# A list-scheduled Fourier and maxout kernel: its plan counts loads, issues and shared PSUM reads in another way

## The chip, the cores and the metric

The kernel runs on one NeuronCore of one Trainium2 chip. The metric is the device time of one execution in microseconds, the median of several runs. PE is TensorE (matmuls), DVE VectorE, ACT ScalarE, POOL GpSimd, SP SyncE; each runs its own instructions in the order in which they stand in its queue.

## The reference

```python
X = np.fft.rfft(x, axis=1)                       # x: 8 x 3072 x 256, float32
Yr = Xr @ w_r - Xi @ w_i + b_r                   # 256 x 256 weights
Yi = Xr @ w_i + Xi @ w_r + b_i
Y* = sign(Y*) * max(|Y*| - 0.01, 0)
y = np.fft.irfft(Yr + 1j * Yi, n=3072, axis=1)   # float32
x = y.reshape(8 * 3072, 256)
h = max(max(x @ w1, x @ w2), x @ w3)             # 256 x 768 weights
return h @ w_out                                 # 768 x 256
```

## The kernel before

For each of 8 batches the Fourier transform is done as matmuls in stages. **Stage a** loads a piece `xq` of x (8 pieces a batch), takes its largest value (`mxx`, DVE, which sets a scale later), multiplies by a small DFT table (`pa`), copies to `aq` (ACT) and writes it to DRAM (`a_d`). **Steps k = 0 to 11** load a slab `aj` of `a_d`, split it into a float16 pair `ah`, `al`, multiply (`px`), split that (`tt`, and a sum `s`), multiply with w_r and w_i (`py`), add the bias and threshold (`u`, `t`), split (`vp`), transform back (`pz`), copy to `zs` (ACT) and write to DRAM (`z_d`). **The second part** takes 8 chunks c a batch: load `zp` from `z_d` (one buffer; GpSimd clears its middle rows, then SP issues two loads), split it into `zh` (ACT) and `zl` (DVE), multiply (`pi`), split into `yh`, `yl`. Then, for six slices f of a chunk, the maxout layer: `pu` (two PSUM tiles of 12 matmuls in all; w3 is taken off the other two weights beforehand and added back in `pd`), `c1` (ACT, called c in the profile), `h32` (DVE, h in the profile), the pair `hh` (ACT then DVE), and `pd`, from which `o` is copied out by ACT and written by DMAs that ACT issues. Nearly every product is three float16 matmuls (`mm3`: lines 304 to 306 before); L298 and L299 are the helper that splits.

A **slot** is one (batch, chunk, slice), 48 a batch and 384 in all. Slots are counted here by c1: "c1 number 98" is batch 2, chunk 0, slice 2. The second part of batch b runs beside the first part of batch b + 1; `at` and `run_until` place a step's functions in the slots.

The code is traced in that written order, and what comes after the mark (from slot 6 on) is then put in another order by a planner. `gather` groups instructions into operations with a cost (`busy`) and a time until others may use the result (`wait`), from the tables `COST`. `link` finds what each operation needs (`needs`) or must stand behind (`behind`): who wrote what it reads, and who used a buffer that it takes over (`BUFS` gives the number of buffers). `arrange` plays all of it through, and picks for DVE and ACT the ready operation that is due first, for PE the first ready one within 40 in the written order; POOL, and before the change SP, stay as written. The order that comes out is fixed by dependencies that cost no semaphore. No time of this planner is used in this document: it fixes the order, and the chip decides how long things take.

In the plan before, `link` made only the **first** writer of a reused buffer wait for the buffer's former users. For `xq` and `zp` that is GpSimd's memset, so their loads waited for nothing there. A DMA that ACT issues counted 0.13 us of ACT. ACT and DVE reads of one PSUM tile did not wait for each other in the plan (the program itself does order them).

Of the kernel before, what the change touches and what calls it, by code (L numbers as in the profile page):

```python
# [24 lines left out]
def dft_tables():  # L25
# [57 lines left out]
    def halves(v, scale):  # L83
# [20 lines left out]
    "DVE": {  # L104
        "h32": 0.475, "hh": 0.475, "yl": 0.467, "zl": 1.2, "t": 0.45, "mxu": 0.6, "mxx": 0.6, "vp": 0.66, "s": 0.36,
        "al": 0.67, ("u", 256): 0.49, ("u", 512): 0.605, ("tt", 512): 0.605, ("tt", 256): 0.34,
    },
    "Activation": {
        "c1": 0.43, "hh": 0.43, "yh": 0.37, "o": 0.36, "ah": 0.61, "zh": 1.04, "zs": 0.6, "vp": 0.6, "s": 0.37,
        "cs": 0.37, "aq": 0.493, ("tt", 512): 0.48, ("tt", 256): 0.3,  # L110
    },
}


class Op:
    def __init__(self, engine, label, key=None):
        self.engine, self.label, self.key = engine, label, key
        self.ins, self.reads, self.writes, self.busy = [], set(), set(), 0.0


def gather(traced):
    ops, last = [], None
    for i in traced:
        ends = [[a for a in v if getattr(a, "bass_ap", None) is not None] for v in (i.ins, i.outs)]
        if not ends[1]:
            continue
        reads, writes = ([a.bass_ap.tensor.name for a in v] for v in ends)
        sizes = [int(np.prod([c for _, c in a.ap[1:]])) for v in ends for a in v]
        engine, n = str(i.engine).split(".")[-1], sizes[-1]
        label = writes[0].rsplit("_", 1)[0]  # L130
        if engine == "PE":
            key = label if label in ("pi", "pa", "pd") else writes[0]
            if last is None or last.key != key:
                last = Op(engine, label, key)
                last.busy = {"pi": 0.19, "pa": 0.1}.get(label, 0.0)
                ops.append(last)
            plain = ends[0][0].dtype == F32
            cost = (4 if plain else 1) * n / 2400 + 0.0025
            last.busy += {"pi": cost / 2, "pa": 0.23}.get(label, cost)
            last.wait = last.busy + 0.22  # L140
            op = last
# [12 lines left out]
        op.writes |= set(writes)  # L154
    return ops


def link(ops):
    wrote, read, taken, used, opened = defaultdict(list), defaultdict(list), defaultdict(list), set(), {}
    reuse = []  # L160
    for k, o in enumerate(ops):
        o.needs, o.behind = {w for t in o.reads for w in wrote[t]}, set()
        for t in o.writes:
            name = t.rsplit("_", 1)[0]
            if name not in ("a_d", "z_d"):
                o.needs |= set(read[t])
            tag = TAGS.get(name, name)
            if t not in used:
                used.add(t)
# [3 lines left out]
                if len(taken[tag]) > BUFS.get(tag, 2):  # L173
                    reuse.append((k, taken[tag][-1 - BUFS.get(tag, 2)]))
# [25 lines left out]
def arrange(ops, first):  # L200
# [6 lines left out]
    left, ready = [len(kept & (o.needs | o.behind)) for o in ops], [0.0] * len(ops)  # L207
    free, order, open_ = defaultdict(float), defaultdict(list), defaultdict(list)
    written = defaultdict(list)
    for k, o in enumerate(ops):  # L210
# [4 lines left out]
    done, count = defaultdict(int), len(ops) - len(kept)  # L215
    ran = [False] * len(ops)
    while count < len(ops):
        best = None
        for e, c in open_.items():
            if not c:  # L220
                continue
            w = written[e]
            if e in ("DVE", "Activation"):
                t = max(free[e], min(ready[k] for k in c))
                k = min((k for k in c if ready[k] <= t + 1e-9), key=lambda k: (ops[k].due, k))
            elif e == "PE":
                c = [k for k in c if k <= w[min(done[e] + 40, len(w) - 1)]]
# [3 lines left out]
                k = min(now) if now else min(c, key=lambda k: (ready[k], k))  # L231
                t = max(free[e], ready[k])
            else:
                k = w[done[e]]
                if k not in c:
                    continue
                t = max(free[e], ready[k])
            if best is None or t < best[0]:
                best = t, e, k
        t, e, k = best  # L240
        if e in ("DVE", "Activation"):
            c, end = open_[e], t + ops[k].busy
            soon = [j for j in c if t < ready[j] < end and ops[j].due < min(end, ops[k].due)]
            if soon:
                until = min(ready[j] for j in soon)
                fits = [j for j in c if ready[j] <= t + 1e-9 and t + ops[j].busy <= until + 0.03]
                if not fits:
                    free[e] = until
# [10 lines left out]
        for u in o.users + o.followers:  # L259
            left[u] -= 1  # L260
            ready[u] = max(ready[u], t + (o.wait + 0.05 if k in ops[u].needs else 0.01))
            if not left[u]:
# [5 lines left out]
def fourier_maxout_kernel(  # L268
# [759 lines left out]
    for b in range(NB):  # L1028
        for c in range(NCH):
            nxt = (b, c + 1) if c + 1 < NCH else (b + 1, 0) if b + 1 < NB else None  # L1030
            for f in range(NF):
                if (b, c, f) == (0, 1, 0):
                    mark = len(nc.cur_bb.bb.instructions)
                hh = up(y, f)
# [22 lines left out]
    traced = nc.cur_bb.bb.instructions  # L1057
    early = gather(traced[:mark])
    ops = early + gather(traced[mark:])
    link(ops)  # L1060
# [40 lines left out]
```

## Time and profile before

| | us |
|---|---|
| median of 3 runs | 1877.86 (1877.79 to 1878.32) |
| the profiled execution | 1877.33 |
| its span, first to last instruction | 1875.5 |
| PE busy in it | 1783.5 |
| DVE, ACT, POOL busy | 1304.0, 945.7, 127.9 |
| granted TensorE clock, mean | 0.992 |

The span is what the profiler saw of the instructions; the time around it is 1.8 us. Times in rows count from the start of the span. Idle time of an engine is given with what ended it ("<-"). PE overlaps matmuls, so each one's length is longer than the distance to the next.

### The profile page before, as it was taken

To read this page: it belongs to the slowest core of one execution; us is meant where nothing else is said; L and a number is where in the kernel's file an instruction comes from. 1 tells how busy PE (TensorE), PEld (TensorE's weight loads), DVE (VectorE), ACT (ScalarE), POOL (GpSimd) and SP (SyncE) were. 2 spreads that over 40 slices of the span, in tenths; PEclk is the share of its full clock that TensorE was granted. 3 is DMA by queue.
4 is the path that set the end of the run, shared out by engine and by line. 5 is a ranking of instruction groups with operands and counts; after the bars stand their busy time and mean duration, and the time that the engine had idled before them with its cause. 6 is when DMAs were issued, how large, how long until landed. Compare 5 with 4: busy or idle time off the path is not lost.

```text
span 1875.5 us, 39465 instructions
## 1 busy us (share of the span) xinstructions
PE 1783.5 (95%) x16071; PEld 1260.2 (67%) x16071; DVE 1304.0 (70%) x2580; ACT 945.7 (50%) x1930; POOL 127.9 (7%) x183
## 2 busy tenths in 40 slices
PE   5979999999999999999999999999999999999899
PEld 2755667766776666667677667766667677776666
DVE  1896798658875678757786588766877578863443
ACT  2344565455555455455554455545555555543443
POOL 0001100100010000100001000000001000000000
PEclk9989999999999999999999999999999999999999
DMA  8634432342324232242322433133232312111100
GB/s 261 212 102 118 113 100 64 100 108 73 99 66 116 71 91 79 63 116 79 86 71 74 117 84 91 57 101 103 78 93 65 94 57 63 49 57 44 43 27 26
DMA packets 116600, 164.71 MB, mean 88 GB/s; under 512 B 13137, under 2 KB 88914, under 8 KB 116418
## 3 DMA queue, kind: packets, MB, share of 16 engines
q1 hardware_dynamic: 54466, 86.66, 17.2%
q10 hardware_dynamic: 61952, 75.52, 13.5%
q8 instruction: 126, 2.06, 0.5%
q14 instruction: 56, 0.46, 0.1%
HBM read 86.64 MB, written 75.50 MB: 86 GB/s over the span
## 4 chain that ended last, share of the span: by engine, by line
PE 39%; issue 23%; DMA 9%; DVE 9%; ACT 4%; POOL 3%; SPq 1%; POOLq 0%; ACTq 0%; DVEq 0%
PE pu L304 6%; DMA zp<-z_d 6%; PE pu L306 6%; PE pu L305 6%; PE pd L306 4%; PE pd L304 4%; PE pd L305 4%; DMA xq<-in_x_dram 2%; DVE u L791 2%; PE py L304 2%; POOL zp L882 2%; PE py L306 1%; PE py L305 1%; PE pa L608 1%; DVE h L930 1%
## 5 line engine op out<-in xcount | busy, mean ns | idle before, releaser
L304 PE MATMUL pu<-yh,wuh 128*128 128x384 f16 x1536 | 504.1, 328 | 36.4 <-ACT c L928 33.8
L305 PE MATMUL pu<-yl,wuh 128*128 128x384 f16 x1536 | 503.7, 328 | 0.0
L306 PE MATMUL pu<-yh,wul 128*128 128x384 f16 x1536 | 503.6, 328 | 0.0
L298 ACT ACTIVATE hh<-h 128x384 f16<-128x384 f32 x384 | 200.0, 521 | 391.0 <-DVE h L930 378.6
L930 DVE TENSOR_TENSOR h<-pu,c 128x384 f32<-128x384 f32 x384 | 213.1, 555 | 195.1 <-PE pu L306 154.6
L306 PE MATMUL pd<-woh,hh 128*128 128x256 f16 x1152 | 314.7, 273 | 7.8 <-DVE hh L299 6.9
L304 PE MATMUL pd<-woh,hh 128*128 128x256 f16 x1152 | 314.6, 273 | 2.5 <-ACT hh L298 0.9
L305 PE MATMUL pd<-wol,hh 128*128 128x256 f16 x1152 | 314.3, 273 | 0.0
L299 DVE SCALAR_TENSOR_TENSOR hh<-h,hh 128x384 f16<-128x384 f32 x384 | 213.2, 555 | 102.7 <-ACT hh L298 100.4
L928 ACT ACTIVATE c<-pu 128x384 f32<-128x384 f32 x384 | 187.7, 489 | 138.4 <-PE pu L306 132.2
L305 PEld LDWEIGHTS <-wuh 128*128 128x128 f16 x1536 | 151.0, 98 | 129.3 <-issue 48.9
L304 PEld LDWEIGHTS <-wuh 128*128 128x128 f16 x1536 | 151.0, 98 | 111.6 <-issue 29.8
L306 PEld LDWEIGHTS <-wul 128*128 128x128 f16 x1536 | 150.9, 98 | 101.2 <-issue 2.9
L791 DVE SCALAR_TENSOR_TENSOR u<-py,s1x,cs 64x256 f32<-64x256 f32 x308 | 148.5, 482 | 15.8 <-ACT cs L802 10.7
L304 PE MATMUL py<-wch,tt 128*128 128x256 f16 x504 | 137.7, 273 | 0.0
L305 PE MATMUL py<-wcl,tt 128*128 128x256 f16 x504 | 137.4, 273 | 0.0
L306 PE MATMUL py<-wch,tt 128*128 128x256 f16 x504 | 137.4, 273 | 0.0
L304 PEld LDWEIGHTS <-hh 128*128 128x128 f16 x1152 | 112.8, 98 | 36.2 <-issue 5.0
L306 PEld LDWEIGHTS <-hh 128*128 128x128 f16 x1152 | 112.7, 98 | 33.8 <-DVE hh L299 20.3
L305 PEld LDWEIGHTS <-hh 128*128 128x128 f16 x1152 | 112.8, 98 | 31.8 <-issue 4.6
L594 DVE TENSOR_REDUCE mxx<-xq 112x1 f32<-112x512 f32 x112 | 74.3, 679 | 65.6 <-DMA xq<-in_x_dram 65.2
L299 DVE SCALAR_TENSOR_TENSOR zl<-zp,s0u,zh 112x1024 f16<-112x1024 f32 x64 | 81.9, 1279 | 47.6 <-ACT zh L298 47.6
(184 smaller groups left out, 2935.2 us busy)
## 6 DMA issues: line engine op xcount, KB each, us to landing
aj<-a_d SPq DMA_DIRECT2D x96, 256.0 KB, 3.1
z_d<-zs ACTq DMA_DIRECT2D x96, 256.0 KB, 2.2
zp<-z_d SPq DMA_DIRECT2D x128, 192.0 KB, 3.8
out_dram<-o ACTq DMA_DIRECT2D x192, 128.0 KB, 2.3
a_d<-aq ACTq DMA_DIRECT2D x124, 192.0 KB, 2.9
xq<-in_x_dram SPq DMA_DIRECT2D x120, 192.0 KB, 4.2
rw<-in_moe_w_dram SPq DMA_DIRECT2D x12, 384.0 KB, 6.5
xr<-in_x_dram SPq DMA_DIRECT2D x16, 96.0 KB, 3.7
```

The source lines that it names most:

```text
L298: nc.scalar.activation(out=hi, in_=src, func=AF.Copy, scale=scale)
L299: nc.vector.scalar_tensor_tensor(out=lo, in0=src, scalar=scale, in1=h, op0=ALU.mult, op1=ALU.subtract)
L304: nc.tensor.matmul(o, lh, rh, start=start, stop=False, **kw)
L305: nc.tensor.matmul(o, lh, rl, start=False, stop=False, **kw)
L306: nc.tensor.matmul(o, ll, rh, start=False, stop=stop, **kw)
L594: nc.vector.tensor_reduce(out=batch(b, "x")[0:XR, 2 * q4 + i:2 * q4 + i + 1], in_=xp, axis=AX.X, op=ALU.max, apply_absolute_value=True,)
L608: nc.tensor.matmul(pa[r][64 * c:64 * c + 64], fr[rows], xs[c][rows], start=True, stop=True)
L791: nc.vector.scalar_tensor_tensor(out=u[64 * c:64 * c + 64, j], in0=pk[r], scalar=inv[r], in1=c1[r], op0=ALU.mult, op1=ALU.add,)
L882: nc.gpsimd.memset(zq[32:64], 0.0)
L928: nc.scalar.activation(out=c1, in_=pu[0], func=AF.Relu)
L930: nc.vector.tensor_tensor(out=h32, in0=pu[1], in1=c1, op=ALU.max)
```

## The change

The planner's picture is changed, and one spacing; the operations are the same, with as many instructions on each engine. A load now waits in the plan for all users of the buffer that it takes over, and those of `xq` and `zp` also for the memset. All DMAs share one carrier (`moved`): 2.0 us after issue, one after the other at 150 KB/us, 1.5 us to the landing. SP's loads are ordered like the operations of DVE and ACT. An issue takes its sequencer 0.36 us, or 0.58 us close behind another. ACT and DVE reads of one PSUM tile are kept in order in the plan. Margins on costs are smaller (1.08 to 1.04, and the delays behind them). From batch 2 on, steps stand 2.7 slots apart in place of 2.8.

```diff
+MARGIN = 1.04
+ISSUE, LEAD, RATE, LAND = (0.36, 0.58), 2.0, 150e3, 1.5
...
-            last.wait = last.busy + 0.22
+            last.wait = last.busy + 0.26
...
-                op.busy, op.wait = 0.13 if engine == "Activation" else 0.4, 4.5 if label == "xq" else 3.5
+                op.dma, op.busy, op.wait = True, ISSUE[0], 4.5 if label in ("xq", "zp") else 3.5
...
-                op.busy = 1.08 * (table.get((label, n)) or table.get(label) or 0.08 + n / 960)
-                op.wait = op.busy + 0.18
+                op.busy = MARGIN * (table.get((label, n)) or table.get(label) or 0.08 + n / 960)
+                op.wait = op.busy + 0.1
...
+        for t in o.reads:
+            if TAGS.get(t.rsplit("_", 1)[0]) in ("ff", "up", "dn"):
+                o.needs |= {r for r in read[t] if ops[r].engine != o.engine}
...
+            if name in ("xq", "zp"):
+                o.needs |= {w for w in wrote[t] if not ops[w].dma}
...
-    for k, old in reuse:
-        ops[k].needs |= set(wrote[old] + read[old])
...
+        for t in {old[t] for t in o.writes} - {None}:
+            o.needs |= set(wrote[t] + read[t])
...
+    def start(e, k):
+        return max(issue[e], ready[k], 0.0 if ops[k].dma else free[e])
...
-            if e in ("DVE", "Activation"):
-                t = max(free[e], min(ready[k] for k in c))
-                k = min((k for k in c if ready[k] <= t + 1e-9), key=lambda k: (ops[k].due, k))
-            elif e == "PE":
+            if e == "PE":
...
+            else:
+                t = min(start(e, k) for k in c)
+                k = min((k for k in c if start(e, k) <= t + 1e-9), key=lambda k: (ops[k].due, k))
...
-        free[e] = t + o.busy
+        if o.dma:
+            issue[e] = t + ISSUE[t - issued < ISSUE[1]]
+            issued, moved = t, max(moved, t + LEAD) + o.bytes / RATE
+            wait = moved + LAND - t
+        else:
+            free[e], issue[e], wait = t + o.busy, t, o.wait
...
-        with tc.issue_after(st["ld"].ins) if q >= NCH + 2 else nullcontext():
+        with tc.issue_after(st["ld"].ins) if q >= NCH + 2 and "mark" not in st else nullcontext():
...
-            p = 8 + 2.2 * (k + 2) if b == 1 else (b - 1) * SLOTS + 2.8 * (k + 2)
+            p = 8 + 2.2 * (k + 2) if b == 1 else (b - 1) * SLOTS + 2.7 * (k + 2)
```

Line numbers grow by 16 in the part of the code after the planner. In the rows of the order below, buffer numbers follow the tracing, so one and the same load can carry another number in the other program.

**ScalarE at the start of batch 2.** Before, from c1 number 98 on; `zp_8074` is the load for chunk 2 of batch 2, whose buffer was that of `zp_7728`:

```order
L928 ACTIVATE c1_7746<-pu_7732 128x384
L298 ACTIVATE hh_7714<-h32_7712 128x384
L298 ACTIVATE yh_7857<-pi_7859 128x96x4
L298 ACTIVATE zh_8192<-zp_8074,s0u_7401 112x1024
L298 ACTIVATE yh_7857<-pi_7860 128x96x4
L928 ACTIVATE c1_7779<-pu_7765 128x384
L298 ACTIVATE hh_7750<-h32_7748 128x384
```

And now, from the next c1 (number 99) to number 101:

```order
L944 ACTIVATE c1_7779<-pu_7765 128x384
L314 ACTIVATE hh_7783<-h32_7781 128x384
L944 ACTIVATE c1_7835<-pu_7821 128x384
L314 ACTIVATE hh_7839<-h32_7837 128x384
L314 ACTIVATE yh_7857<-pi_7859 128x96x4
L314 ACTIVATE tt_7926<-px_7913 128x2x256
L314 ACTIVATE yh_7857<-pi_7860 128x96x4
L314 ACTIVATE ah_8173<-aj_8015,s0x_7494 128x512
L944 ACTIVATE c1_7948<-pu_7934 128x384
L739 ACTIVATE s_7929<-px_7913 128x256
L314 ACTIVATE zh_8192<-zp_8074,s0u_7369 112x1024
L314 ACTIVATE hh_7952<-h32_7950 128x384
```

The split `zh` of that load moved from behind c1 number 98 to behind number 101, and `s` no longer stands directly behind the `tt` of the same `px`: five rows lie between.

**VectorE in batch 2, chunk 2, slices 3 to 5.** Before, behind h32 number 111; `mxx` reads a piece of x just loaded, `tt` is the low half whose PSUM tile ScalarE's `s` reads next:

```order
L299 SCALAR_TENSOR_TENSOR hh_8588<-h32_8586,hh_8588 128x384
L749 TENSOR_TENSOR u_8546<-u_8546,t_8559 128x512
L827 TENSOR_REDUCE mxu_8312<-u_8546 128x1
L594 TENSOR_REDUCE mxx_7762<-xq_9067 112x1
L299 SCALAR_TENSOR_TENSOR tt_8635<-px_8622,tt_8635 128x2x256
L930 TENSOR_TENSOR h32_8663<-pu_8654,c1_8661 128x384
L724 SCALAR_TENSOR_TENSOR s_8638<-px_8622,s_8638 128x256
```

And now, from h32 number 112 (the same tile 8663) on; `xq_9089` is that same piece of x:

```order
L946 TENSOR_TENSOR h32_8663<-pu_8654,c1_8661 128x384
L310 TENSOR_TENSOR tt_8620<-s_8623,tt_8620 128x2x128
L315 SCALAR_TENSOR_TENSOR hh_8665<-h32_8663,hh_8665 128x384
L315 SCALAR_TENSOR_TENSOR yl_8684<-pi_8685,yh_8683 128x96x4
L315 SCALAR_TENSOR_TENSOR zl_9094<-zp_8962,s0u_7369,zh_9093 112x1024
L315 SCALAR_TENSOR_TENSOR yl_8684<-pi_8686,yh_8683 128x96x4
L807 SCALAR_TENSOR_TENSOR u_8758<-py_8743,s1x_7498,cs_8756 64x256 x2
L946 TENSOR_TENSOR h32_8790<-pu_8781,c1_8788 128x384
L807 SCALAR_TENSOR_TENSOR u_8758<-py_8761,s1x_7498,cs_8756 64x256 x2
L315 SCALAR_TENSOR_TENSOR hh_8792<-h32_8790,hh_8792 128x384
L830 TENSOR_TENSOR u_8758<-u_8758,bias_86 128x512
L610 TENSOR_REDUCE mxx_7762<-xq_9089 112x1
```

The `mxx` moved from before h32 number 112 to behind number 113, and nothing that waits for a load stands ahead of the `tt`.

**SP where batch 2's first z load is issued** (`zp_7409`, from `z_d_5236`). Before:

```order
L884 DMA zp_7048<-z_d_2324 48x1024 x2
L586 DMA xq_7159<-in_x_dram 48x2x512 x2
L884 DMA zp_7409<-z_d_5236 48x1024 x2
L586 DMA xq_7513<-in_x_dram 48x2x512 x2
L632 DMA aj_7694<-a_d_4608 128x2x256
```

And now:

```order
L900 DMA zp_7052<-z_d_2324 48x1024 x2
L602 DMA xq_7166<-in_x_dram 48x2x512 x2
L602 DMA xq_7513<-in_x_dram 48x2x512 x2
L900 DMA zp_7409<-z_d_5236 48x1024 x2
L648 DMA aj_7694<-a_d_4608 128x2x256
```

The load of `xq_7513` went ahead of the batch's first z load. On POOL the order is the same in both programs.

## Rows read from the trace of the kernel before

**Rows 1.** The page's head and its part 1: busy us (share of the span) and instructions of each engine.

```profile
span 1875.5 us, 39465 instructions
...
PE 1783.5 (95%) x16071; PEld 1260.2 (67%) x16071; DVE 1304.0 (70%) x2580; ACT 945.7 (50%) x1930; POOL 127.9 (7%) x183
```

**Rows 2.** PE's waits from 180 us to the end: engine, what it was to write, its line, what ended the wait; us in total, times, longest us.

```profile
PE pu L304 <- ACT c L928: 33.8, 22, 3.4
PE pd L306 <- DVE hh L299: 6.4, 24, 0.4
PE pa L608 <- DMA xq<-in_x_dram: 1.5, 1, 1.5
PE pu L304 <- DVE h L930: 1.2, 4, 0.5
PE pi L906 <- DVE zl L299: 1.1, 1, 1.1
PE pd L304 <- ACT hh L298: 0.9, 2, 0.6
PE pd L304 <- ACT o L957: 0.8, 5, 0.2
PE pt L374 <- DVE col L372: 0.7, 1, 0.7
PE pi L906 <- ACT zh L298: 0.6, 1, 0.6
```

**Rows 3.** Waits of ACT and of DVE from 180 us on, the same columns.

```profile
ACT s L723 <- DVE tt L299: 123.0, 77, 4.9
ACT zh L298 <- DMA zp<-z_d: 53.8, 17, 4.3
...
DVE mxx L594 <- DMA xq<-in_x_dram: 61.7, 24, 4.0
```

**Rows 4.** The timeline around c1 number 98 and 99: start us, us, engine, line, operation, out<-in, shapes, count, [idle time before, what ended it].

```profile
602.68 1.27 DVE L299 SCALAR_TENSOR_TENSOR zl<-zp,s0u,zh 112x1024 f16<-112x1024 f32 x1
...
604.02 0.94 POOL L882 MEMSET zp<- 32x1024 f32 x1 [9.39 <-DVE zl L299]
...
604.99 0.79 SPq L884 DMA_DIRECT2D zp<-z_d  x2
...
611.01 1.15 ACT L298 ACTIVATE zh<-zp,s0u 112x1024 f16<-112x1024 f32 x1 [3.94 <-DMA zp<-z_d]
...
612.43 0.48 ACT L928 ACTIVATE c<-pu 128x384 f32<-128x384 f32 x1
...
612.97 0.32 PE L304 MATMUL pu<-yh,wuh 128*128 128x384 f16 x1 [3.04 <-ACT c L928]
613.13 0.32 PE L305 MATMUL pu<-yl,wuh 128*128 128x384 f16 x1
```

**Rows 5.** The timeline around c1 number 112, the same columns.

```profile
668.82 0.80 SPq L586 DMA_DIRECT2D xq<-in_x_dram  x2
...
672.94 0.69 DVE L594 TENSOR_REDUCE mxx<-xq 112x1 f32<-112x512 f32 x1 [3.89 <-DMA xq<-in_x_dram]
...
673.54 0.68 DVE L299 SCALAR_TENSOR_TENSOR tt<-px,tt 128x512 f16<-128x512 f32 x1
...
674.26 0.38 ACT L723 ACTIVATE s<-px 128x256 f32<-128x256 f32 x1 [4.78 <-DVE tt L299]
674.54 0.48 ACT L928 ACTIVATE c<-pu 128x384 f32<-128x384 f32 x1
...
675.08 0.32 PE L304 MATMUL pu<-yh,wuh 128*128 128x384 f16 x1 [0.85 <-ACT c L928]
```

**Rows 6.** The timeline around c1 number 133 (batch 2, chunk 6, slice 1), the same columns.

```profile
769.54 0.41 POOL L732 TENSOR_SCALAR tt<-tt 128x256 f16<-128x256 f16 x1 [39.78 <-ACT tt L298]
...
772.18 0.94 POOL L882 MEMSET zp<- 32x1024 f32 x1
...
773.15 1.97 SPq L884 DMA_DIRECT2D zp<-z_d  x2
...
778.41 1.15 ACT L298 ACTIVATE zh<-zp,s0u 112x1024 f16<-112x1024 f32 x1 [4.24 <-DMA out_dram<-o]
...
779.98 0.32 PE L304 MATMUL pu<-yh,wuh 128*128 128x384 f16 x1 [2.09 <-ACT c L928]
```

**Rows 7.** PE's waits from 1702 us on (batch 7, beside which no first part runs), the columns of Rows 2.

```profile
PE pu L304 <- ACT c L928: 7.7, 4, 2.5
```

**Rows 8.** Busy us (and instructions) of PE, PEld, DVE, ACT and POOL in four stretches, then the granted TensorE clock, the DMA share and GB/s.

```profile
837.06:840.47 3.41, 2.92 (x10) 1.36 (x10) 3.29 (x6) 1.45 (x4) 0.94 (x1) 0.50 0.01 1
...
1697.21:1700.63 3.42, 3.42 (x13) 1.56 (x12) 0.64 (x2) 0.66 (x2) 0.00 (x0) 0.50 0.65 135
...
1755.24:1758.65 3.41, 3.41 (x15) 1.98 (x14) 1.05 (x3) 0.90 (x2) 0.09 (x1) 0.50 0.48 119
188.52:191.93 3.41, 3.41 (x15) 1.45 (x17) 2.02 (x4) 1.84 (x5) 0.94 (x1) 0.50 0.33 78
```

**Rows 9.** The last issues of the program, on ACT's sequencer, from its timeline.

```profile
1871.10 1.85 ACTq L958 DMA_DIRECT2D out_dram<-o  x3
```

**Rows 10.** A wait of SP's queue over the whole span: what it was to issue, what ended the wait; us, times, longest.

```profile
SPq L586 <- POOL xq L584: 144.8, 28, 8.2
```

**Rows 11.** The page's part 5, one group: busy us, mean ns of one | idle time before, and what ended it.

```profile
L928 ACT ACTIVATE c<-pu 128x384 f32<-128x384 f32 x384 | 187.7, 489 | 138.4 <-PE pu L306 132.2
```

More of the change, by code (lines that the diff above doesn't have):

```diff
@@ L104 @@
     "DVE": {
-        "h32": 0.475, "hh": 0.475, "yl": 0.467, "zl": 1.2, "t": 0.45, "mxu": 0.6, "mxx": 0.6, "vp": 0.66, "s": 0.36,
+        "h32": 0.47, "hh": 0.475, "yl": 0.467, "zl": 1.2, "t": 0.45, "mxu": 0.6, "mxx": 0.6, "vp": 0.66, "s": 0.34,
         "al": 0.67, ("u", 256): 0.49, ("u", 512): 0.605, ("tt", 512): 0.605, ("tt", 256): 0.34,
@@ L108 @@
     "Activation": {
-        "c1": 0.43, "hh": 0.43, "yh": 0.37, "o": 0.36, "ah": 0.61, "zh": 1.04, "zs": 0.6, "vp": 0.6, "s": 0.37,
-        "cs": 0.37, "aq": 0.493, ("tt", 512): 0.48, ("tt", 256): 0.3,
-    },
-}
+        "c1": 0.42, "hh": 0.43, "yh": 0.37, "o": 0.36, "ah": 0.61, "zh": 1.04, "zs": 0.6, "vp": 0.6, "s": 0.37,
+        "cs": 0.37, "aq": 0.5, ("tt", 512): 0.48, ("tt", 256): 0.3,
+    },
+}
+MARGIN = 1.04
+ISSUE, LEAD, RATE, LAND = (0.36, 0.58), 2.0, 150e3, 1.5
 class Op:
     def __init__(self, engine, label, key=None):
-        self.engine, self.label, self.key = engine, label, key
+        self.engine, self.label, self.key, self.dma = engine, label, key, False
         self.ins, self.reads, self.writes, self.busy = [], set(), set(), 0.0
@@ L145, in gather @@
             if i.opcode == "DMACopy":
-                op.busy, op.wait = 0.13 if engine == "Activation" else 0.4, 4.5 if label == "xq" else 3.5
+                op.dma, op.busy, op.wait = True, ISSUE[0], 4.5 if label in ("xq", "zp") else 3.5
+                op.bytes = max(
+                    int(np.prod([c for _, c in a.ap])) * (2 if a.dtype == F16 else 4) for v in ends for a in v
+                )
             else:
@@ L158, in link @@
 def link(ops):
-    wrote, read, taken, used, opened = defaultdict(list), defaultdict(list), defaultdict(list), set(), {}
-    reuse = []
+    wrote, read, taken, opened, old = defaultdict(list), defaultdict(list), defaultdict(list), {}, {}
     for k, o in enumerate(ops):
         o.needs, o.behind = {w for t in o.reads for w in wrote[t]}, set()
+        for t in o.reads:
+            if TAGS.get(t.rsplit("_", 1)[0]) in ("ff", "up", "dn"):
+                o.needs |= {r for r in read[t] if ops[r].engine != o.engine}
         for t in o.writes:
@@ L166, in link @@
                 o.needs |= set(read[t])
-            tag = TAGS.get(name, name)
-            if t not in used:
-                used.add(t)
+            if name in ("xq", "zp"):
+                o.needs |= {w for w in wrote[t] if not ops[w].dma}
+            if t not in old:
+                tag = TAGS.get(name, name)
+                n = BUFS.get(tag, 2)
                 taken[tag].append(t)
@@ L172, in link @@
                 opened[tag] = k
-                if len(taken[tag]) > BUFS.get(tag, 2):
-                    reuse.append((k, taken[tag][-1 - BUFS.get(tag, 2)]))
+                old[t] = taken[tag][-1 - n] if len(taken[tag]) > n else None
         for t in o.reads:
@@ L207, in arrange @@
     left, ready = [len(kept & (o.needs | o.behind)) for o in ops], [0.0] * len(ops)
-    free, order, open_ = defaultdict(float), defaultdict(list), defaultdict(list)
-    written = defaultdict(list)
+    free, issue, order, open_ = defaultdict(float), defaultdict(float), defaultdict(list), defaultdict(list)
+    written, issued, moved = defaultdict(list), -9.0, 0.0
     for k, o in enumerate(ops):
@@ L231, in arrange @@
                 k = min(now) if now else min(c, key=lambda k: (ready[k], k))
-                t = max(free[e], ready[k])
-            else:
+            elif e == "Pool":
                 k = w[done[e]]
@@ L236, in arrange @@
                     continue
-                t = max(free[e], ready[k])
+            else:
+                t = min(start(e, k) for k in c)
+                k = min((k for k in c if start(e, k) <= t + 1e-9), key=lambda k: (ops[k].due, k))
+            t = start(e, k)
             if best is None or t < best[0]:
@@ L242, in arrange @@
             c, end = open_[e], t + ops[k].busy
-            soon = [j for j in c if t < ready[j] < end and ops[j].due < min(end, ops[k].due)]
+            soon = [j for j in c if t < start(e, j) < end - 0.03 and ops[j].due < min(end, ops[k].due)]
             if soon:
-                until = min(ready[j] for j in soon)
-                fits = [j for j in c if ready[j] <= t + 1e-9 and t + ops[j].busy <= until + 0.03]
+                until = min(start(e, j) for j in soon)
+                fits = [j for j in c if start(e, j) <= t + 1e-9 and t + ops[j].busy <= until + 0.03]
                 if not fits:
-                    free[e] = until
+                    issue[e] = until
                     continue
@@ L260, in arrange @@
             left[u] -= 1
-            ready[u] = max(ready[u], t + (o.wait + 0.05 if k in ops[u].needs else 0.01))
+            ready[u] = max(ready[u], t + (wait if k in ops[u].needs else 0.01))
             if not left[u]:
@@ L1032, in fourier_maxout_kernel @@
                 if (b, c, f) == (0, 1, 0):
-                    mark = len(nc.cur_bb.bb.instructions)
+                    st["mark"] = len(nc.cur_bb.bb.instructions)
                 hh = up(y, f)
@@ L1057, in fourier_maxout_kernel @@
     traced = nc.cur_bb.bb.instructions
-    early = gather(traced[:mark])
-    ops = early + gather(traced[mark:])
+    early = gather(traced[:st["mark"]])
+    ops = early + gather(traced[st["mark"]:])
     link(ops)
```

## The prediction

> **What bounds the kernel now.** I read the busy times first: PE works in 95% of the span [rows 1], so a gain must come from the 92.0 us (1875.5 - 1783.5) in which it does not. Next its waits. About half of that time lies before 180 us, where the code is traced before the mark and the order stays as it was. From 180 us on there are nine kinds of wait, 47.0 us in 61 pieces; one kind has 33.8 us of it: the first `pu` of a slice waits until ACT has made `c` of the slice before and so freed the PSUM buffer [rows 2].
>
> ACT is busy only half of the span [rows 1], so `c` is late because something ahead of it in ACT's order waits. ACT's own waits name two such things: `s` behind DVE's `tt`, 123.0 us, and `zh` on the landing of `zp`, 53.8 us. DVE has one of the kind: `mxx` on the landing of `xq`, 61.7 us [rows 3]. Most of these 238 us cost nothing, because PE has other work meanwhile; the timeline shows where they reach it, at three places that come back in most batches, and in batch 7.
>
> - c1 number 98: `zl` frees the buffer, GpSimd clears it, SP issues the two loads, and ACT already stands at the next `zh`; it waits 3.94 us with `c` behind it, and PE then 3.04 [rows 4].
> - Number 112: DVE stands at `mxx` for 3.89 us until `xq` lands. `tt` is behind it, ACT's `s` waits 4.78 us for `tt`, `c` is behind `s`, PE waits 0.85 [rows 5].
> - Number 133: GpSimd clears `zp` only behind step 11's `tt`, the loads go out at 773.15, `zh` waits 4.24, PE 2.09 [rows 6]. The row names a DMA of `o`; the loads of `zp` in front of it are what `zh` reads.
> - Batch 7: four waits, 7.7 us [rows 7].
>
> **A wait costs more than its row says.** Two `pu` matmuls start 0.16 us apart while each lasts 0.32 [rows 4]. A wait is counted from the end of the matmul before it, so each loses 0.16 us beyond its row: 61 pieces, 9.8 us.
>
> **The clock.** In four stretches the granted clock is 0.50, the lower level of 1.2 GHz: 837.06, 1697.21, 1755.24 and 188.52, with 2.92 + 3.42 + 3.41 + 3.41 = 13.2 us of PE work at half speed, so 6.6 us lost [rows 8]. PE had stood still just before or at the start of each, on `c`, `zl` and `col`. As a further 6.6 us the four belong to the stalls. The Trainium skill (TensorE: Matmul & The Clock Gate, section "What's actually happening") advises for modelling to take such a ramp as under 1% of a typical span and not to fit it to counts. The trace agrees on the size (6.6 us of 1875.5 is 0.4%); taken as advice it strikes the clock term below, and the sum would come out at 1838 us.
>
> **The change part by part.**
>
> *Loads wait for former users and the memset; one carrier.* In the order before, 17 of the `zh` that the planner places stand at most two c1 behind the `zl` that frees their buffer; now one does, 12 stand three and the other 49 four or more behind it. From `zl` to `zh` the chip took 611.01 - 602.68 = 8.3 us [rows 4]. A slot with no other PE work in it holds 12 matmuls of 0.16 us and 9 of two thirds of that (256 columns against 384), so 2.9 us, an estimate from the same rows; three slots are 8.7 us. So the load has landed when ACT comes to `zh`. For `mxx`, in 15 cases it stood in the same slot as the `pa` matmuls that free the buffer; in those it now stands two or three slots later. Both moves stand in the order's rows of ACT and DVE.
>
> *ACT and DVE reads of one PSUM tile in order.* 75 of 77 `s` stood directly behind their `tt`, and ACT waited 1.6 us each (123.0/77). Now one does; the rest have two to six rows between.
>
> *Spacing 2.7.* Step 11's split moves one slot earlier on ACT (c1 number 131 to 130) and chunk 7's `zh` one later (132 to 133), which widens the third place by two slots, at least 5.8 us against the 4.24 us wait [rows 6]. No row bears on a cost of it: the same steps lie closer together where PE has work anyway, and if that cover were gone it would show as more waits of the second kind of [rows 2].
>
> *Issues count, SP ordered, smaller margins.* I take these together, in the new waits below.
>
> The sum, from the chip's rows:
> 1. All 22 waits on `c` go: 33.8 + 22 x 0.16 = 37.3 us.
> 2. Of the 24 short waits of `pd` for the low half of `hh`, half go, those that follow a stall while DVE catches up: half of 6.4 + 24 x 0.16 = 10.2, so 5.1 us. Between none and all, I take the middle.
> 3. The single waits on `xq`, `col`, `zl` and `zh`: 1.5 + 0.7 + 1.1 + 0.6 + 4 x 0.16 = 4.5 us. The `pa` in question stands three slots later, the `zh` of batch 7's first chunk one earlier.
> 4. Clock: the three later stretches, half of 9.75 us: 4.9 us.
> 5. Tail: the last three issues follow the last copy and take 1.85 us [rows 9]. Now one is issued before that copy: 0.6 us.
>
> Together 52.4 us. Against it stand new waits, which no row of before can show. Below they are nothing. Above I take all the small ones of today that no late load explains, 10.2 us for `hh` and the three other kinds (1.2 + 0.9 + 0.8 and 11 x 0.16 = 4.7): 14.9 us. Half of it, 7.4 us, since two slots of batch 7 now have `hh` behind the next slot's `c`, but 29 slots in place of 54 begin otherwise than `pu`, `pu`, `pd`. Net 45.0 us: 1877.3 - 45.0 = 1832.3 for the profiled execution, which lies 0.5 under the median; so **1833 us**.
>
> **Rivals.**
>
> *Half of it (1850 to 1873 us).* The chip's loads land later than the plan has it, since several are issued close together, and ACT or DVE waits again, at other places. Terms 1 and 4 then come to about half: 52.4 - 21 - 7.4 = 24, so 1854. For it speak the landings themselves, 5.3 us from issue to `zh` in one place and 6.0 in another [rows 4, 6]; against it that 49 of 62 `zh` have a slot or more beyond the 8.3 us.
>
> *Slower: the batch's first z load behind an x load.* On SP the two loads of `xq_7513` now stand ahead of `zp_7409`, and nothing of a batch's second part can start without the latter. SP waits for GpSimd's memset of `xq` 28 times, 5.2 us in the mean and at most 8.2 [rows 10]. If each of seven batches paid the longest, 57 us would be added: 1890 us. From 6.4 us a batch (45/7) on the change is a loss. Against it: that memset needs only a `pa` of two pieces earlier, and the `zh` of a batch's first chunk stands a slot earlier than before in five batches.
>
> *Slower in small steps*, the same side: the tight margins make one slot in four pay a wait like today's for `hh` (0.27 + 0.16 = 0.43): 96 x 0.43 = 41 us, near no gain. `c` lasts 0.489 us [rows 11]; the plan gives it 0.42 x 1.04 + 0.1 = 0.54 before its result counts. It isn't short there.
>
> *No change:* PE's order is set by its own work and what goes on ACT comes back on PE. 1877 us. Against it: the 33.8 us are real standstill, named by row.
>
> *More than forecast:* all of [rows 2] goes, with the clock and the tail: 47.0 + 9.8 + 6.6 + 0.6 = 64 us, 1814.
>
> **How the numbers follow.** My forecast 0.80; more than forecast, below 1821, 0.05; half of it 0.09; no change 0.02; slower, either way, 0.04. The range goes from 1821 (new waits near nothing, and term 2 whole) to 1850, up to the half case. A change under 0.2%, 3.8 us, can't be told from none: faster 0.94, same 0.02, slower 0.04.
>
> **What would show it.** Right: PE's waits on `c` after 180 us fall from 33.8 us to a few; ACT's `zh` on `zp` and DVE's `mxx` on `xq` to under 10 us each; ACT's `s` on `tt` to under 20; PE busy falls by about the clock's 5 us; at most one stretch of half clock is left after 180 us. Wrong in term 2: `pd` on `hh` stays above 6 us. Wrong in the rival's way: `pi` or `pu` waits for `zh`, `zl` or `yh` at the batch starts, or a wait on `xq`'s landing in PE's list. If the waits on `c` are gone and the time has not fallen by 35 us, the loss per wait or the price of new waits was misjudged.

## The result

The changed kernel takes 1818.0 us (median of 5, 1816.85 to 1818.15) against 1878.32 for the kernel before on the same chip: a ratio of 0.967, 95% interval 0.9652 to 0.9687. That is 60.3 us less, 15.0 us under the forecast of 1833 and 3.0 us under the low end of its range. The direction and the main mechanism were right; the size was not, because PE lost more to the late loads than its list of waits shows. The profiled execution took 1817.62 us, 59.7 less than that of before.

The head and part 1 of the page of the changed kernel, to be read against [rows 1]:

```profile
span 1815.8 us, 39428 instructions
...
PE 1766.3 (97%) x16071; PEld 1264.7 (70%) x16071; DVE 1309.2 (72%) x2580; ACT 979.7 (54%) x1930; POOL 125.6 (7%) x183
```

PE executes the same 16071 matmuls and is "busy" 17.2 us less. PE's waits from 180 us to the end, in the columns of [rows 2] (the writing helper is now at L320 to L322, the splits at L314 and L315):

```profile
PE pu L320 <- ACT yh L314: 4.7, 1, 4.7
PE pi L922 <- ACT ah L314: 1.2, 1, 1.2
PE pi L922 <- DVE ex L396: 0.4, 1, 0.4
PE pu L320 <- ACT c L944: 0.4, 1, 0.4
PE pi L922 <- ACT aq L626: 0.3, 1, 0.3
PE pi L922 <- DVE zl L315: 0.2, 1, 0.2
```

Where there were 47.0 us in 61 pieces there are 7.2 in 6, nearly all of it of kinds that [rows 2] does not have. Of ACT's and DVE's rows in [rows 3], `zh` on the landing of `zp` and `mxx` on that of `xq` are no longer among their waits, and `s` on `tt` fell from 123.0 us to 4.2:

```profile
ACT s L739 <- DVE tt L315: 4.2, 13, 0.7
```

Two stretches, each from c1 number 48 to 96 and from 240 to 288, show what a batch costs: busy us and instructions of PE, PEld, DVE, ACT and POOL, then the clock, the DMA share and GB/s. Before:

```profile
378.90:600.60 221.70, 215.47 (x2011) 151.74 (x2010) 161.89 (x314) 117.31 (x242) 17.13 (x24) 1.00 0.32 87
...
1269.00:1489.10 220.10, 214.49 (x2003) 151.57 (x2002) 160.54 (x312) 116.04 (x240) 15.31 (x22) 1.00 0.30 84
```

And after; the last two rows are the two stretches at half clock that the changed kernel has after 180 us:

```profile
384.90:597.90 213.00, 213.00 (x2013) 152.69 (x2012) 162.72 (x314) 122.65 (x241) 16.68 (x24) 1.00 0.33 91
...
1233.00:1445.60 212.60, 212.60 (x2011) 152.39 (x2009) 161.62 (x312) 122.46 (x242) 14.92 (x22) 1.00 0.31 87
204.34:211.16 6.82, 4.35 (x14) 1.91 (x14) 0.96 (x3) 0.98 (x2) 0.00 (x0) 0.50 0.83 241
235.06:238.47 3.41, 3.40 (x65) 3.03 (x65) 3.31 (x6) 2.38 (x5) 0.00 (x0) 0.50 0.95 269
```

PE is busy for the whole batch: 213.00 of 213.00 us. The first row of each also shows that at c1 number 48 the changed kernel is still 6.0 us *behind* (384.90 against 378.90), so it gains later (8.7 and 7.5 us in these two, 56.5 us in the six batches from number 48 to 336), and has lost something before. Where it lost it shows in the first 19 copies `c` of each trace (first and last start in us); before, then after:

```profile
L928 ACT ACTIVATE c<-pu x19: 484/490/516, 142.2 to 231.9; 128x384 f32<-128x384 f32 x19
```

```profile
L944 ACT ACTIVATE c<-pu x19: 469/490/511, 144.9 to 241.5; 128x384 f32<-128x384 f32 x19
```

c1 number 0 is 2.7 us later and number 18 is 9.6. The 2.7 us need not be the change's: in a second trace of the changed kernel number 0 comes at 142.6. In between lies the new wait of 4.7 us. The timeline after, around it:

```profile
185.25 1.20 SPq L900 DMA_DIRECT2D zp<-z_d  x2
...
198.75 1.15 ACT L314 ACTIVATE zh<-zp,s0u 112x1024 f16<-112x1024 f32 x1
...
203.58 0.48 ACT L314 ACTIVATE yh<-pi 128x384 f16<-128x384 f32 x1
203.71 2.39 ACTq L628 DMA_DIRECT2D a_d<-aq  x2
...
206.15 0.49 ACT L314 ACTIVATE yh<-pi 128x384 f16<-128x384 f32 x1 [2.09 <-DMA zp<-z_d]
...
206.70 0.48 PE L320 MATMUL pu<-yh,wuh 128*128 128x384 f16 x1 [4.70 <-ACT yh L314]
```

The load of `zp` was issued at 185.25, and `zh` stands at 198.75 without a wait of its own: the order put other work of ACT ahead of it. So `pi`, `yh` and the first `pu` of the chunk come late. The row of the second `yh` names the landing of a `zp`, which `yh` does not read. Directly ahead of it on ACT stand two DMA issues, 2.39 us in one row. The first takes 0.83 us; then nothing happens until 205.80, when the second goes out in 0.31. By its record in the trace that second issue waits for a semaphore that it shares with a `zp` load issued by SP at 202.24, whose last signal comes at 205.78. So some 1.3 us of the 2.39 are a wait at a landing after all.

### The profile page after: what moved, and what is told of

Same layout as the page of the kernel before. It is cut to its first block, busy times and chain, and to the rows that moved or that the text cites. A ratio compares the mean times of both kernels' runs of the same rounds, so it can differ in the third digit from the quotient of the medians.

```text
span 1815.8 us, 39428 instructions
## 1 busy us (share of the span) xinstructions
PE 1766.3 (97%) x16071; PEld 1264.7 (70%) x16071; DVE 1309.2 (72%) x2580; ACT 979.7 (54%) x1930; POOL 125.6 (7%) x183
## 3 DMA queue, kind: packets, MB, share of 16 engines
q1 hardware_dynamic: 54466, 86.66, 17.9%
## 4 chain that ended last, share of the span: by engine, by line
PE 92%; DVE 3%; DMA 3%; ACT 1%; issue 0%; SPq 0%; ACTq 0%; POOL 0%; DVEq 0%
PE pu L320 14%; PE pu L321 14%; PE pu L322 14%; PE pd L322 9%; PE pd L320 9%; PE pd L321 9%; PE pa L624 3%; PE py L320 3%; PE py L322 3%; PE py L321 3%; PE pi L922 2%; PE px L320 1%; PE pz L320 1%; PE px L322 1%; PE px L321 1%; PE pz L321 1%
## 5 line engine op out<-in xcount | busy, mean ns | idle before, releaser
L320 PE MATMUL pu<-yh,wuh 128*128 128x384 f16 x1536 | 503.4, 328 | 5.4 <-ACT yh L314 4.7
L322 PE MATMUL pu<-yh,wul 128*128 128x384 f16 x1536 | 502.8, 327 | 0.0
L314 ACT ACTIVATE hh<-h 128x384 f16<-128x384 f32 x384 | 200.5, 522 | 326.4 <-DVE h L946 322.9
L322 PE MATMUL pd<-woh,hh 128*128 128x256 f16 x1152 | 314.0, 273 | 0.9 <-DVE hh L315 0.9
L320 PE MATMUL pd<-woh,hh 128*128 128x256 f16 x1152 | 314.1, 273 | 0.2
L315 DVE SCALAR_TENSOR_TENSOR hh<-h,hh 128x384 f16<-128x384 f32 x384 | 213.6, 556 | 95.1 <-ACT hh L314 93.3
L320 PEld LDWEIGHTS <-wuh 128*128 128x128 f16 x1536 | 150.5, 98 | 113.7 <-issue 32.9
L322 PEld LDWEIGHTS <-wul 128*128 128x128 f16 x1536 | 150.4, 98 | 100.9 <-issue 2.0
L320 PE MATMUL py<-wch,tt 128*128 128x256 f16 x504 | 137.9, 274 | 0.0
L322 PE MATMUL py<-wch,tt 128*128 128x256 f16 x504 | 137.6, 273 | 0.1
L320 PEld LDWEIGHTS <-hh 128*128 128x128 f16 x1152 | 112.5, 98 | 33.3 <-issue 2.4
L322 PEld LDWEIGHTS <-hh 128*128 128x128 f16 x1152 | 112.5, 98 | 15.0 <-DVE hh L315 1.7
L315 DVE SCALAR_TENSOR_TENSOR yl<-pi,yh 128x384 f16<-128x384 f32 x128 | 70.7, 554 | 56.5 <-ACT yh L314 55.2
L898 POOL MEMSET zp<- 32x1024 f32 x64 | 60.3, 943 | 717.9 <-DVE zl L315 714.7
```

The lines of the kernel that those rows point to most:

```text
L314: nc.scalar.activation(out=hi, in_=src, func=AF.Copy, scale=scale)
L315: nc.vector.scalar_tensor_tensor(out=lo, in0=src, scalar=scale, in1=h, op0=ALU.mult, op1=ALU.subtract)
L320: nc.tensor.matmul(o, lh, rh, start=start, stop=False, **kw)
L322: nc.tensor.matmul(o, ll, rh, start=False, stop=stop, **kw)
L898: nc.gpsimd.memset(zq[32:64], 0.0)
```

## The experiments

After the result three things had to be told apart. **Loads:** the loads that wait in the plan move `zh` and `mxx` away from landings, and that is the gain. **Reads:** the gain comes from keeping `s` away from `tt`, the largest row of [rows 3]. **Carrier:** the shared carrier and SP's order made the loss before c1 number 48. Ratios are against the kernel before on the same chip, with 95% intervals; its medians there were 1878.63 us (beside the loads alone, the reads alone, both together, and the old spacing), 1882.07 (beside the kernel without load waits, the fixed landing, SP as written, and the faster carrier) and 1881.81 (beside each load by itself, the old margins, and the changed kernel again).

### The loads alone, put into the kernel before

```diff
-                if len(taken[tag]) > BUFS.get(tag, 2):
-                    reuse.append((k, taken[tag][-1 - BUFS.get(tag, 2)]))
+                old[t] = taken[tag][-1 - BUFS.get(tag, 2)] if len(taken[tag]) > BUFS.get(tag, 2) else None
+            if name in ("xq", "zp"):
+                o.needs |= {w for w in wrote[t] if ops[w].engine == "Pool"}
...
-    for k, old in reuse:
-        ops[k].needs |= set(wrote[old] + read[old])
+    for o in ops:
+        for t in {old[t] for t in o.writes} - {None}:
+            o.needs |= set(wrote[t] + read[t])
```

> The kernel before with one part of the change in its planner: a load waits in the plan for all users of its buffer, and for the memset. Late-load theory (the stalls come from ACT and DVE standing at a load that the plan thought landed): PE's waits on c fall from 33.8 us to under 15, ACT's zh on zp from 53.8 to under 15 and DVE's mxx on xq from 61.7 to under 15; the time falls by 25 to 40 us, to 1838 to 1853. Rival (the order of ACT's and DVE's reads of one PSUM tile is what mattered, since s behind tt was ACT's largest wait): s stays directly behind tt, the waits on c stay above 20 us and the time falls by less than 12 us.

Measured: 1808.85 us, ratio 0.9627 (0.9607 to 0.9646): 69.8 us less, more than the whole change and more than was expected. Part 1 of its page, its PE waits from 180 us (all of them), and one of ACT's; its lines are two higher than before:

```profile
PE 1762.0 (98%) x16071; PEld 1262.4 (70%) x16071; DVE 1307.2 (72%) x2580; ACT 958.9 (53%) x1930; POOL 128.0 (7%) x183
```

```profile
PE pu L306 <- ACT c L930: 1.0, 3, 0.5
PE pd L308 <- DVE hh L301: 0.8, 4, 0.2
PE pd L306 <- ACT hh L300: 0.6, 1, 0.6
...
ACT s L725 <- DVE tt L301: 80.3, 77, 2.8
```

ACT still waits 80.3 us for `tt`, and PE has 2.4 us in all its listed waits. A wait of 80 us cost next to nothing here; those of 54 and 62 us were the price.

### The order of reads alone, and both together

```diff
+        for t in o.reads:
+            if TAGS.get(t.rsplit("_", 1)[0]) in ("ff", "up", "dn"):
+                o.needs |= {r for r in read[t] if ops[r].engine != o.engine}
```

> The kernel before with another part alone: reads of one PSUM tile by ACT and DVE are kept in order in the plan. Late-load theory: ACT's s on tt falls from 123 us to under 30, yet zh still stands at its loads (above 45 us) and the time falls by at most 12 us, to 1866 or more. Rival (PSUM reads): 25 us or more, to 1853 or less.

Measured: 1866.69 us, ratio 0.9931 (0.9908 to 0.9955), 11.9 us less. Its waits, PE's first, then two of ACT's:

```profile
PE pu L307 <- ACT c L931: 29.1, 17, 3.2
...
ACT zh L301 <- DMA zp<-z_d: 53.4, 18, 4.8
...
ACT s L726 <- DVE tt L302: 21.7, 12, 3.4
```

and one more of PE's, with DVE's wait at `mxx`:

```profile
PE pd L309 <- DVE hh L302: 0.4, 2, 0.2
...
DVE mxx L597 <- DMA xq<-in_x_dram: 75.0, 24, 4.4
```

The edit does what it says: `s` behind `tt` falls from 123.0 to 21.7. The waits at landings stay (`zh` 53.4 us against 53.8, `mxx` 75.0 against 61.7), and with them most of the waits on `c`. PE's listed waits on the low half of `hh` go all the same, from 6.4 to 0.4 us; in their place PE waits 3.2 us for `s` and 3.0 for `yl`. So what DVE has in its order behind `mxx` decides which tile comes late. Now this edit together with the one above (its other lines are as there):

```diff
+        for t in o.reads:
+            if TAGS.get(t.rsplit("_", 1)[0]) in ("ff", "up", "dn"):
+                o.needs |= {r for r in read[t] if ops[r].engine != o.engine}
...
+            if name in ("xq", "zp"):
+                o.needs |= {w for w in wrote[t] if ops[w].engine == "Pool"}
```

> Both of these parts on the kernel before; the carrier, SP's order, ACT's issues, margins and spacing stay as before. Late-load theory: most of the 60 us is there, 40 to 55 us, so 1823 to 1838. Rival (the plan's accuracy, that is issues, margins and the carrier, makes the many short waits go): at most 35 us, 1843 or more, and pd's waits on hh stay above 5 us.

Measured: 1807.78 us, ratio 0.9617 (0.9592 to 0.9641). That is below the range that was expected, and 1.1 us under the loads alone, which cannot be told from nothing. Once the landings are out of the way the order of reads has nothing left to give that shows.

### The changed kernel without its load waits

```diff
-            if name in ("xq", "zp"):
-                o.needs |= {w for w in wrote[t] if not ops[w].dma}
...
+                first[t] = k
...
-        for t in {old[t] for t in o.writes} - {None}:
+        for t in {old[t] for t in o.writes if first[t] == k} - {None}:
...
-            elif e == "Pool":
+            elif e in ("Pool", "SP"):
```

> The changed kernel without its waits of loads for former users and the memset, and with SP in the written order, as before. Late-load theory: ACT's zh on zp and DVE's mxx on xq come back to above 30 us each, PE's waits on c to above 15 us, 1840 to 1862. Rival (the other parts carry half of the gain): 1822 to 1835.

Measured: 1878.06 us (10 runs), ratio 0.9981 (0.9967 to 0.9995): 4.0 us are left of the gain, less than either theory had. The waits of PE, ACT and DVE that matter:

```profile
PE pu L319 <- DVE h L945: 19.5, 25, 2.4
PE pu L319 <- ACT c L943: 12.2, 14, 2.4
...
ACT zh L313 <- DMA zp<-z_d: 45.0, 10, 5.4
...
DVE mxx L609 <- DMA xq<-in_x_dram: 82.7, 22, 4.9
```

The same two landings stall ACT and DVE again, and PE stands about as long as in [rows 2] (44.8 us in all its listed waits), more at `h` than at `c`. SP's written order, which this kernel has too, is not the cause (it is tried alone below). So the load waits are enough for the gain and, inside the change with SP in the written order, needed for it.

### Each load by itself

Only `zp`, as a difference to the loads alone:

```diff
-            if name in ("xq", "zp"):
+            if name == "zp":
...
-        for t in {old[t] for t in o.writes} - {None}:
+        late = {t for t in o.writes if t.startswith("xq_") and o.engine == "SP"}
+        for t in {old[t] for t in o.writes - late} - {None}:
```

> The kernel before, where in the plan only the loads of zp wait for the buffer's former users and the memset, not those of xq. If the two stalls add up, as my places had them (zh at c1 numbers 98 and 133 and in batch 7: 29 of the 33.8 us), the time falls by 40 to 55 us, 1823 to 1838, and DVE's mxx on xq stays above 45 us. If zh is all, within 4 us of the 1809 us with both. If the late x loads cost more than my 4.3 us at number 112, in waits too short for the list, it falls by less than 40.

Measured: 1839.37 us, ratio 0.9772 (0.9758 to 0.9787), 42.4 us less. And only `xq`:

```diff
-            if name in ("xq", "zp"):
+            if name == "xq":
...
-        for t in {old[t] for t in o.writes} - {None}:
+        late = {t for t in o.writes if t.startswith("zp_") and o.engine == "SP"}
+        for t in {old[t] for t in o.writes - late} - {None}:
```

> The same with only the loads of xq waiting. Adding up: the time falls by 8 to 25 us, 1853 to 1870; mxx on xq under 15 us, zh on zp stays above 45. If mxx costs nothing beyond its row: at most 7 us.

Measured: 1854.52 us, ratio 0.9852 (0.9837 to 0.9867), 27.3 us less, somewhat more than was expected. The two add up to 69.7, the gain of both together (69.8). What each leaves shows whose waits were whose. PE's waits, and those of its weight loads (PEld) on the low half of `hh`, with `zp` alone:

```profile
PE pu L307 <- ACT c L931: 5.7, 9, 1.0
PE pd L309 <- DVE hh L302: 5.5, 20, 0.4
...
PEld L309 <- DVE hh L302: 15.4, 36, 0.7
```

with `xq` alone:

```profile
PE pu L307 <- ACT c L931: 30.5, 19, 3.4
...
PE pd L309 <- DVE hh L302: 1.0, 5, 0.2
...
PEld L309 <- DVE hh L302: 5.0, 15, 0.5
```

The waits on `c` belong to `zp`: ACT stands at `zh`. Most of the small waits on `hh` belong to `xq`: DVE stands at `mxx`, and in the order before it is late with `hh` in the slots that follow. In the weight loads' rows 45 such stalls (19.2 us) were there before; `zp` alone leaves 36 of them, `xq` alone 15. `xq` alone gained 27.3 us though [rows 2] has only 6.4 + 1.5 us under names that go with it. In all kinds together PE's list is 12.8 us shorter with it (32 pieces, so 17.9 with 0.16 each); most of the rest lies in stalls too short for a row, which are counted below.

### What lost the first 10 us

The changed kernel with a fixed time to the landing in the plan, in place of one carrier for all:

```diff
-            issued, moved = t, max(moved, t + LEAD) + o.bytes / RATE
-            wait = moved + LAND - t
+            issued, wait = t, o.wait + 0.05
```

> The changed kernel, but in the plan each DMA lands a fixed time after its issue (4.55 us for xq and zp, 3.55 for the others) and none waits for another. It tests where the changed kernel loses its 9 us to the loads-alone kernel, slots 9 to 18 (c1 number 18 comes 96.6 us after number 0, there 84.3). Carrier theory (the plan makes the many DMAs behind the mark queue up and holds zh and pa back): c1 number 18 comes 84 to 88 us after number 0, PE's waits on yh and ah near 205 and 235 us are gone, 1807 to 1811. Rival (the free order of SP's loads does it): 1815 or more, and the wait on yh stays.

Measured: 1806.96 us, ratio 0.961 (0.9589 to 0.9631). c1 number 18 comes 85.3 us after number 0, and PE has no wait on `yh` after 180 us. The changed kernel with SP in the written order:

```diff
-            elif e == "Pool":
+            elif e in ("Pool", "SP"):
```

> The changed kernel with SP's loads in the written order, all else as changed. Carrier theory: the loss in slots 9 to 18 stays, 1815 to 1821. Rival (order of SP's loads): 1807 to 1811.

Measured: 1812.49 us, ratio 0.964 (0.9619 to 0.966). The new wait is still there:

```profile
PE pu L320 <- ACT yh L314: 2.9, 1, 2.9
```

The time lies between the two forecasts. c1 number 18 comes 93.9 us after number 0 (238.8 - 144.9), so of the 12 us lost in these slots some 9 are left, and SP's order made at most a small part of them. The fixed landing says that the carrier made the rest. The changed kernel with a faster carrier:

```diff
-ISSUE, LEAD, RATE, LAND = (0.36, 0.58), 2.0, 150e3, 1.5
+ISSUE, LEAD, RATE, LAND = (0.36, 0.58), 2.0, 400e3, 1.5
```

> The changed kernel with one number changed: the shared carrier moves 400 KB/us in the plan in place of 150. Carrier theory: as with no shared carrier, 1806 to 1811, c1 number 18 at 84 to 88 us after number 0. Rival (150 is about what the chip moves, and a faster carrier in the plan sends zh and mxx ahead of their landings again): zh's waits on zp above 20 us and 1820 or more.

Measured: 1804.13 us (1802.16 to 1805.83), ratio 0.9593 (0.9569 to 0.9616). This is the lowest median of all, clear of both kernels; its interval overlaps those of the fixed landing, the loads alone and both parts together, so from these it can't be told. Its first 19 copies `c`, all its PE waits from 180 us, and the load and split that came late above:

```profile
L944 ACT ACTIVATE c<-pu x19: 473/491/512, 143.8 to 228.6; 128x384 f32<-128x384 f32 x19
```

```profile
PE pu L320 <- ACT c L944: 0.4, 1, 0.4
PE pd L322 <- DVE hh L315: 0.3, 1, 0.3
```

```profile
184.33 1.22 SPq L900 DMA_DIRECT2D zp<-z_d  x2
...
191.24 1.15 ACT L314 ACTIVATE zh<-zp,s0u 112x1024 f16<-112x1024 f32 x1 [1.08 <-DMA zp<-z_d]
```

From the load to `zh` it is 6.9 us here and 13.5 in the changed kernel, and c1 number 18 starts 84.8 us after number 0, not 96.6. At 150 KB/us the plan takes loads that are issued close together to land later than they do (the chip moved 241 and 269 GB/s in the two rows at half clock above), puts other work ahead of what reads them, and PE stands. A landing planned too late costs, as one planned too early does.

### Two edits that show no difference, and the changed kernel again

First the changed kernel with the old spacing:

```diff
-            p = 8 + 2.2 * (k + 2) if b == 1 else (b - 1) * SLOTS + 2.7 * (k + 2)
+            p = 8 + 2.2 * (k + 2) if b == 1 else (b - 1) * SLOTS + 2.8 * (k + 2)
```

> The changed kernel with the steps 2.8 slots apart as before. Late-load theory: the plan knows when chunk 7's load comes, so nothing waits; 1817 to 1822. Rival (the spacing frees the third place): the wait of about 2 us with its 0.16 comes back in 6 batches, 1826 to 1832.

Measured: 1819.1 us, ratio 0.9681 (0.9661 to 0.9701), against 0.967 (0.9652 to 0.9687) for the changed kernel. Then with the old margins (and four old costs):

```diff
-MARGIN = 1.04
+MARGIN = 1.08
...
-            last.wait = last.busy + 0.26
+            last.wait = last.busy + 0.27
...
-                op.wait = op.busy + 0.1
+                op.wait = op.busy + 0.23
```

> The changed kernel with the margins and delays of before (1.08, 0.23 us behind an operation, the old costs). If margins matter for the short waits: 1824 or more, with pd's waits on hh above 3 us. If not: 1814 to 1821.

and beside it, on the same chip, the changed kernel as it is:

> The changed kernel once more, beside the others of this job: 1816 to 1820, so that the 1804 us with the carrier at 400 KB/us are not the chip's.

Measured: 1814.48 us with the old margins, ratio 0.964 (0.9624 to 0.9656), and 1814.55 without, ratio 0.9643 (0.9629 to 0.9658). Neither the spacing nor the margins can be told from no change. The changed kernel's second time is 1.5 us under what was expected; its ratio still lies clear of that with the faster carrier (0.9569 to 0.9616).

The order of reads was not taken out of the changed kernel by itself, nor were the issue costs tried alone.

## Why the prediction was right, and where it was wrong

The working below is for the profiled executions, 1877.33 to 1817.62: 59.7 us.

| step | forecast, us | what the two traces show, us |
|---|---|---|
| 1, waits on `c` | 37.3 | 33.8 in 22 became 0.4 in 1: 33.4 + 21 x 0.16 = 36.8 |
| 2, `pd` on the low half of `hh` | 5.1 | 6.4 in 24 became none: 10.2 |
| 3, single waits | 4.5 | 3.9 in 4 became 0.2 in 1: 4.2 |
| kinds taken for staying (`h`, ACT's `hh`, `o`) | 0 | 2.9 in 11 became none: 4.7 |
| 4, clock | 4.9 | half of 13.2 lost before, half of 4.35 + 3.40 now: 2.7 |
| 5, tail | 0.6 | the last issues take 1.20 for 1.85: 0.65 |
| new waits | -7.4 | `yh`, `ah`, `ex`, `aq`: 6.6 in 4: -7.2 |
| start, up to c1 number 0 | 0 | 142.2 became 144.9: -2.7 |
| sum | 45.0 | 49.4 |
| in no row of PE's list | 0 | 59.7 - 49.4 = 10.3; 8.9 of it counted below |

**What failed first: only listed waits were counted.** "A wait costs more than its row says" went in the right direction, but it was applied to 61 pieces that have a row. PE has more waits, so short that PE's list leaves them out, and the sum put these at nothing. One in the trace of before:

```profile
656.02 0.55 DVE L299 SCALAR_TENSOR_TENSOR hh<-h,hh 128x384 f16<-128x384 f32 x1
...
656.30 0.27 PE L305 MATMUL pd<-wol,hh 128*128 128x256 f16 x1
...
656.63 0.10 PEld L306 LDWEIGHTS <-hh 128*128 128x128 f16 x1 [0.34 <-DVE hh L299]
656.63 0.28 PE L306 MATMUL pd<-woh,hh 128*128 128x256 f16 x1
...
656.75 0.27 PE L304 MATMUL pd<-woh,hh 128*128 128x256 f16 x1
```

Such matmuls start 0.11 to 0.12 us apart (the last two). Here the one at 656.63 starts 0.33 after the one before, behind `hh`, which ends at 656.57. PE lost 0.21 us. But the matmul before it is drawn until 656.57, so PE's own idle time is 0.06 us and the row carries no mark; only the weight load's does. The weight loads' rows count this one, and PE's do not. From 180 us on, before and after:

```profile
PEld L306 <- DVE hh L299: 19.2, 45, 0.7
```

```profile
PEld L322 <- DVE hh L315: 0.3, 1, 0.3
```

There were 45 stalls on that tile, not the 24 of [rows 2]. Nor is it the only tile. Going by the starts of all matmuls from 180 us on, outside the stretches at half clock and the short matmuls of `pi`, `pa` and `pt`, the trace of before has 65 places without a row where a matmul starts more than 0.03 us later than its kind usually does: 10.7 us in all. 21 of them are the `pd` on the low half of `hh` (3.6 us), 28 the first `pu` of a slice behind `h` or `c` (4.5), 10 a `pd` behind ACT's `hh` or `o` (1.8). The changed kernel has 9 such places with 1.8 us. That makes 8.9 of the 10.3 us; the other 1.4 stay open. With `zp` alone 8.4 us of these short stalls are left, with `xq` alone 2.3, so most of them come from DVE standing at `mxx`, as most of the listed ones on `hh` do. The first of the two stretches above shows the same: it lost 6.23 us of idle time and has 8.7 us less; its seven listed waits (5.6 us) are worth 6.7 with their 0.16 each, and some 2.0 us are outside the list.

**What failed second: "Between none and all, I take the middle" (term 2), and leaving the small kinds in.** Both were the same mistake, 5.1 + 4.7 us. The prediction saw DVE stand at `mxx` for 61.7 us [rows 3], and followed it only through `tt`, `s` and `c` at number 112 [rows 5]. The experiments with one load each show that its main way to PE is another: through `hh` and `h`, in small pieces. The reason that term 2 gives (stalls that follow while DVE catches up) was right, and only the half had no row behind it. Had `mxx` been followed to each operation that stands behind it on DVE, there would have been a reason to take term 2 whole.

**The ceiling was too low for the same reason.** "More than forecast: all of [rows 2] goes" gave 64 us; the loads alone gave 69.8 in the medians.

**What was right.** Term 1, within 0.5 us, with the mechanism (loads late in the order; ACT at `zh`, `c` behind it). That the 123.0 us of `s` behind `tt` are not the price: with the loads alone they stand at 80.3 and cost nothing that can be told; the order of reads alone was worth 11.9. Terms 3 and 5 as well. The total of new waits (7.4 forecast, 7.2 found) agrees by luck, since it stood for the wrong place: the prediction looked at PE's slots of batch 7 and those that begin otherwise than `pu`, `pu`, `pd`, and they came in the first 18 slots, from the carrier.

**Clock.** Two stretches at half clock are left after 180 us, where one at most was forecast. None is one of [rows 8]; the first begins 2.4 us before PE's wait of 4.70 us ends. The step that said the stretches go with their stalls held: the stalls came elsewhere, and the stretches too. The Trainium skill (TensorE: Matmul & The Clock Gate, section "What's actually happening") advises not to fit such a ramp and puts it under 1% of a typical span. The trace agrees on the size: half of 4.35 + 3.40 is 3.9 us of 1815.8, or 0.2%. Without the clock term the forecast sum would have been 40.1, further off.

**PE's busy time** was to fall by the clock's 5 us. It fell by 17.2, of which 2.7 is the clock and 55 x 0.16 = 8.8 the restarts of listed waits, which the prediction itself had put between PE's rows but not taken out of its busy time. 5.7 are left; the short stalls without a row account for that much, as most of what each loses is drawn as busy. The Trainium skill (Perfetto Trace Analysis, the note at its head) calls matmul busy time a bad metric because matmuls are pipelined, and its "Summary: the profiler window per engine type" says that a matmul's end is estimated. The traces agree: the same 16071 matmuls are 1783.5, 1766.3 and, with the loads alone, 1762.0 us busy.

**The rivals.** "Half of it" had landings later than the plan; what happened was the reverse, landings earlier than the plan has them. The z load behind an x load did not bite: SP's wait for the memset of `xq` grew, and PE's list has no wait at the start of a batch:

```profile
SPq L602 <- POOL xq L600: 279.5, 38, 16.0
```

The margins did not make slots wait for `hh`: one such stall is left in the weight loads' rows.

## What to carry to other kernels

When an engine that works in order stands at a landing, follow everything that is queued behind it to the engine that bounds, and count short waits too: the list of waits on PE showed 24 where its weight loads showed 45. The quickest ceiling is the busy time itself: look what the same matmuls take in a stretch without a stall (213 us a batch here, against 221.7), since a part of each stall is drawn as busy. In a list schedule, a transfer's landing should be neither too early nor too late: after the first error was mended, the second, a carrier at 150 KB/us, cost some 10 us, and 400 gave the lowest median.

## What the runs showed of the hardware that was not expected

PE can work through a batch of 2013 matmuls without one idle moment in the records (213.00 of 213.00 us), while DVE and ACT are busy 76% and 58% of it (162.72 and 122.65). A matmul is drawn longer than the distance to the next, so a stall under some 0.16 us would not show in that figure.

A DMA issue can make an engine wait for a transfer that it has nothing to do with. On ACT the second of the two issues from 203.71 on waited until 205.80 for a semaphore that a `zp` load of SP was the last to use (last signal at 205.78), and ACT's next operation began only behind that issue, at 206.15. The issues themselves took 0.83 and 0.31 us. In the last microseconds of the program two issues took 1.20 without such a wait between them:

```profile
1812.03 1.20 ACTq L974 DMA_DIRECT2D out_dram<-o  x2
```

What made one issue take 0.31 us and another 0.83 was not tried.
